# Two interleaved attention and MLP layers, forward and backward, on one core: the last dV products of the final stage two steps later, and all w2 and wo row blocks of the layer-0 backward products back on TensorE

## The chip, the core and the metric

The kernel runs on one core of one Trainium2 chip. The metric is the device time in microseconds of one execution. The core has TensorE (PE in the profile, with its weight loads listed apart as PEld), VectorE (DVE), ScalarE (ACT), GpSimd (POOL, which here issues the stores) and SyncE (SP, which issues the loads). Sixteen DMA engines move data between HBM and the on-chip memory; results of TensorE land in PSUM and have to be copied out ("evacuated") by VectorE or ScalarE.

## The reference

Two blocks, attention A and MLP B, are applied twice in turn (A, B, A, B) to one token for a batch of 2, with the same weights and the same key and value caches in both layers. The gradients for x, the caches and all weights and biases are asked for.

```python
def attn(x, K, V, wq, wo):            # x: (2, 1, 1024), 32 query heads, 4 kv heads, 16384 keys of 128
    q = (x @ wq) split into 32 heads
    p = softmax(q K^T / sqrt(128))
    return (p V, heads joined) @ wo

def mlp(x, w1, b1, w2, b2):           # 1024 -> 3584 -> 1024
    return gelu(layernorm(x) @ w1 + b1) @ w2 + b2

x = x + attn(layernorm(x), ...); x = x + mlp(layernorm(x), ...)     # layer 0
x = x + attn(layernorm(x), ...); x = x + mlp(layernorm(x), ...)     # layer 1
out_0 = x
out_1 .. out_9 = vjp(grad_out) for x, K, V, wq, wo, w1, b1, w2, b2
```

dK and dV have the size of the caches: 33.5 MB each, in bf16. They are the bulk of what is written.

## The kernel before

**Layout.** Vectors are kept as columns (128 partitions by number of 128-blocks by the batch of 2). Weights come in chunks of 1 MB (0.9 MB for w1), `LDW` = 4096 bf16 per partition, into a ring of 7 tiles (`NLD`); a tile is loaded again when all that read it are done. For one token a product is a matrix times two columns, so a weight block of 128x128 is the stationary operand and the moving operand is the two columns repeated to a width of 32 (`wide_in`). Where the product is with the transposed weight, the block is first transposed on TensorE (`PE.transpose`, eight blocks of 128x128 into one PSUM bank) and copied out by ScalarE or VectorE (`evac_bf16`). Who copies is decided when the program is built: `pick` compares two running sums of charged costs, `load["A"]` and `load["D"]`, and takes the engine with the smaller one; work that has a fixed engine is charged with `charge`.

**Stages.** The order of instructions on every engine is written out by hand (`manual_schedule`).

1. Layer 0 and layer 1 forward, up to about 460 us.
2. The layer-1 backward steps of w1 and wo, then `attn_bwd` (about 505 to 670 us). It runs in slots `s`; a slot handles a quarter of a chunk of 32x128 keys: transposes of V (`emit_T`), the products for dp (`score`), later the sums for dq. The last cache group is kept on chip, and its V tiles have to be turned in place before its own slots come (from the third group on). The deque `v_turns` holds these 16 turns (8 transposes and one evacuation each); before, one is taken in every third slot (`s % 3 == 2`).
3. The layer-0 backward products (about 670 to 755 us), run by the class `Ahead` for w2 (28 row blocks, `w2b`) and then for wo (32 row blocks, `wob`), with the w1 pass (`w_pass`) between them. `Ahead.row(j)` turns the row block, and for w2 first adds the forward products of layer 1 (L356); `Ahead.products(j)` makes the 8 products with the gradient columns (L372). In this kernel every fifth row block, j = 3, 8, 13, ... (`dotted`; 5 of w2 and 6 of wo), isn't turned. For these the gradient is spread first over all partitions (`Ahead.spread`, L328: 16 transposes of a broadcast column and two evacuations), and VectorE takes one row dot product for each of the two batch columns (`Dots.dot`, L332, with a charge of 1.15). The results go to `dp` and are put in afterwards: L805 in `mlp_hidden_bwd`, L831 in `do_delta`. TensorE's order around it: the sums of the layer norm's backward (`ln_bwd`, L178, with a few rows as a `hook` ahead of them), the spread, the remaining rows. Output 0 is transposed and stored in the midst of the w1 pass (`mid`, after the load of row block 4, L193 to L195).
4. `do_delta(0, ...)` gives the layer-0 gradient at the attention output. With it begins the last stage (about 755 us to the end): dK and dV for both layers, dq of layer 0, and all weight gradients. It runs in macro steps `m` of two slots. The 32 chunks stand in `chunks` (8 groups, four chunks each, `NCH` = 4, `NC` = 32). `k_at` and `v_at` give the macro step at which the dK and the dV product of a chunk begin; each has two halves (`kv_pair`, L1189: 8 matmuls into 4 PSUM banks and 4 evacuations of 128x512), one in that step and one in the next, and after the second half a store of 1 MB on GpSimd's queue. Before, chunk i has its dK begin at 2i - 4 (from i = 4 on) and its dV at 2i - 3, so both halves of both run in the same two steps, and `make_blks` turns the coefficients of both in one PSUM bank with one evacuation. The scores of the last chunk end at m = 56, the sums of its dq at m = 58, and its reduction runs at the end of m = 59; it calls `quarter`, which puts the last 16 weight-gradient units of wq (`dw_units`, L1048: one matmul of width 512 and one evacuation each, two stores) into `late` and the products with wq (L875) into `late_pe`. `step_fill` takes 5 such units per macro step.
5. `attn_in_bwd(0, ...)` and `col_to_row_f32` write output 1, a store of 4 KB, behind all of this.

Of the kernel before, what the change touches and what calls it, by code (L numbers as in the profile page):

```python
# [10 lines left out]
F32 = mybir.dt.float32  # L11
# [12 lines left out]
def kernel(  # L24
# [256 lines left out]
    def w_pass(W, n_in, n_out, name, xT_bf=None, gT_bf=None, mid=None):  # L281
# [10 lines left out]
        for j0, rb in w_chunks(n_in, n_out):  # L292
            wv = w_load(W, j0, rb, n_out)
            if mid is not None and j0 == 4:
                mid()
# [22 lines left out]
    class Dots:  # L318


        def __init__(self, name):
            self.rows = [ktp.tile([128, 2 * NB, 128], BF16, name=name, tag="blk", bufs=2) for _ in range(2)]
            self.junk = wrk.tile([128, D], BF16, name="junk", tag="rowout")

        def spread(self, b, col):
            tp = pt([128, 8, 128], BF16, "dotr")
            for o in range(8):
                PE.transpose(tp[:, o, :], col(o).to_broadcast([128, 128]), ident[:])  # L328
            evac_bf16(self.rows[b][:].rearrange("p a b -> p (a b)"), tp[:].rearrange("p a b -> p (a b)"), 1024)

        def dot(self, w, b, out):
            V.scalar_tensor_tensor(out=self.junk[:], in0=w, scalar=1.0, in1=self.rows[b][:].rearrange("p o d -> p (o d)"),  # L332
                                   op0=ALU.mult, op1=ALU.mult, accum_out=out)
            charge("D", 1.15)

    class Ahead:


        def __init__(self, W, n_in, name, xT_bf=None, fps=None):
            self.W, self.J, self.x, self.fps, self.name = W, n_in // 128, xT_bf, fps, name  # L340
            self.dotted = range(3, self.J, 5)
            self.dp = vec.tile([128, len(self.dotted), 2], F32, name=name + "_dp")
            self.chunks = list(w_chunks(n_in, D))
            self.rows = {}
# [7 lines left out]
        def row(self, j):  # L352
# [5 lines left out]
            if j not in self.dotted:  # L358
                turn(w, lambda: pt([128, 8, 128], BF16, "turn"))

        def spread(self, gT_bf):
            self.dd = Dots(self.name + "_g")
            for b in range(2):
                self.dd.spread(b, lambda o: gT_bf[:, o, b:b + 1])

        def products(self, j, out_ps, gT_bf):
            if j in self.dotted:
                for b in range(2):
                    self.dd.dot(self.rows[j], b, self.dp[:, self.dotted.index(j), b:b + 1])
                return  # L370
# [213 lines left out]
    def attn_bwd(l, do_bf, dqT, dn, groups, ahead):  # L584
# [13 lines left out]
        dd = Dots("dqb")  # L598
        dnp = vec.tile([128, HKV, DJ, 2], F32, name="dnp")

        def dot(kv, n, j, b):
            dd.dot(n[4][j - j % 4][:, j % 4, :], b, dnp[:, kv, j, b:b + 1])
            if b == 1:
                V.tensor_tensor(out=dn[:, j], in0=dn[:, j], in1=dnp[:, kv, j], op=ALU.add)

        def by_dots(kv):
# [4 lines left out]
            for b in range(2):  # L611
                wq_q.append(lambda b=b: dd.spread(b, lambda o: dq_all[:, kv * 8 + o, 2 * l + b:2 * l + b + 1]))
# [60 lines left out]
        while s < len(slots) + 2 or sch.busy():  # L673
            sch.s = s
            if s < len(slots):
# [3 lines left out]
                else:  # L679
# [3 lines left out]
                    if s % 3 == 2 and v_turns:  # L683
# [104 lines left out]
    def mlp_hidden_bwd(l, dhps, ahead=None):  # L788
# [15 lines left out]
        if ahead is not None:  # L804
            V.tensor_tensor(out=dh_all[:, 3:FJ:5, lsl(l)], in0=d1[:, 3:FJ:5], in1=ahead.dp[:], op=ALU.mult)  # L805
# [17 lines left out]
    def do_delta(l, dops, ahead=None):  # L823
        sv = saved[f"a{l}"]
        dof = wrk.tile([128, G, 8], F32, name="dof")
        for b in range(2):
            V.tensor_tensor(out=dof[:, b * HKV:(b + 1) * HKV, :].rearrange("p k r -> p (k r)"), in0=dops[:, :, b],
                            in1=sv["rbc"][:, b * HKV:(b + 1) * HKV, :].rearrange("p k r -> p (k r)"), op=ALU.mult)
            if ahead is not None:
                r_ = sv["rbc"][:, b * HKV:(b + 1) * HKV, :].rearrange("p k r -> p (k r)")  # L830
                V.tensor_tensor(out=dof[:, b * HKV:(b + 1) * HKV, :].rearrange("p k r -> p (k r)")[:, 3:HQ:5],  # L831
                                in0=ahead.dp[:, :, b], in1=r_[:, 3:HQ:5], op=ALU.mult)
# [97 lines left out]
    w2b.spread(gM_all[:, :, lsl(0)])  # L930
# [5 lines left out]
    mlp_hidden_bwd(0, pairs(dhps, FJ), w2b)  # L936
# [450 lines left out]
```

## Time and profile before

| what | value |
|---|---|
| time, median of 7 runs | 1173.96 us (1169.58 to 1176.09) |
| time of the profiled execution | 1174.01 us |
| span of the profiled execution | 1172.2 us, mean granted clock 0.825 |
| busy: PE / DVE / ACT | 961.4 us (82%) / 639.0 us (55%) / 562.6 us (48%) |
| moved by DMA | 449.30 MB, mean 383 GB/s |
| DMA share in the last stage, 830 to 1140 us | 1.00 or more in every 10 us |
| first instruction of `do_delta(0)` (L827) | 752.17 us |
| last dq ready (L1238) | 1147.39 us |
| store of output 1 issued (L195) | 1168.10 us |

The profiled execution took 0.05 us more than the median. Its span runs from the first to the last instruction, 1.8 us less than its time. A line of the timeline gives the start, the duration, the engine, the source line, what is written from what, the shapes, the number of instructions merged, and in brackets how long the engine had been idle and what released it.

### The profile page before, as it was taken

Reading aid. Unit: us, or ns where it says so; the run is one execution under the profiler, and the core shown is the slowest. Engines: PE = TensorE matmul, PEld = TensorE weight load, DVE = VectorE, ACT = ScalarE, POOL = GpSimd, SP = SyncE. Lnnn points to the kernel's source line nnn. Section 1 sums busy time; section 2 is a strip of 40 time slices with the busy share of each in tenths; the row PEclk is TensorE's granted clock in tenths of the full one; section 3 lists DMA queues with packets and bytes.
Section 4 is the critical chain, followed back from the end, with each engine's and each line's share of the span. In section 5 each row is a group of like instructions: output and inputs, shape, how many; then the busy total and the mean of one; then the engine's idle time right before and its main releaser. Section 6 shows DMA issues by size and latency. Waiting matters only on the chain. (4 is left out here: it accounts for less than half of the span.)

```text
span 1172.2 us, 39963 instructions
## 1 busy us (share of the span) xinstructions
PE 961.4 (82%) x17565; PEld 735.7 (63%) x17565; DVE 639.0 (55%) x1342; ACT 562.6 (48%) x1412; POOL 63.9 (5%) x113
## 2 busy tenths in 40 slices
PE   4888895488879876899986798688898988999786
PEld 3867673487767755887765697555555554555452
DVE  1535351133535423454844455758868867786774
ACT  0544351022535420344453454367767856686673
POOL 0000000000000000000000000001111111111111
PEclk9979795597989875999997889788859967796785
DMA  9999999998999989989899889668999999999995
GB/s 369 418 420 418 419 420 396 396 348 366 418 420 413 417 314 419 392 338 406 358 412 411 330 320 348 253 242 332 401 420 413 415 420 416 420 421 418 424 414 237
DMA packets 89130, 449.30 MB, mean 383 GB/s; under 512 B 7026, under 2 KB 7026, under 8 KB 49788
## 3 DMA queue, kind: packets, MB, share of 16 engines
q1 hardware_dynamic: 72204, 348.17, 74.3%
q0 software_dynamic: 16752, 98.59, 20.4%
q8 instruction: 137, 2.24, 0.8%
q14 instruction: 37, 0.30, 0.1%
HBM read 348.14 MB, written 98.58 MB: 381 GB/s over the span
## 5 line engine op out<-in xcount | busy, mean ns | idle before, releaser
L148 ACT COPY kT<-tp 128x512 int32<-128x512 int32 x206 | 121.0, 587 | 256.5 <-PE tp L411 242.2
L151 DVE COPY kT<-tp 128x1024 bf16<-128x1024 bf16 x162 | 110.8, 691 | 116.6 <-PE tp L411 105.0
L411 PE MATMUL tp<-ident,kv_K 128*128 128x128 bf16 x1728 | 145.7, 234 | 4.2 <-DMA kv_K<-in_A_k_cache_dram 4.0
L411 PEld LDWEIGHTS <-kv_K 128*128 128x128 bf16 x1728 | 110.6, 104 | 5.1 <-DMA kv_K<-in_A_k_cache_dram 4.5
L159 DVE CAST big<-xm 128x512 bf16<-128x512 f32 (+1 forms) x137 | 89.4, 686 | 26.1 <-PE xm L1189 11.3
L156 ACT CAST big<-xm 128x512 bf16<-128x512 f32 (+1 forms) x160 | 87.1, 593 | 24.8 <-PE xm L1048 13.5
L564 PEld LDWEIGHTS <-kT 128*128 128x128 bf16 x2048 | 76.6, 98 | 28.1 <-issue 22.4
L564 PE MATMUL sc<-qT_bf,kT 128*128 128x8 bf16 x2048 | 92.1, 171 | 0.4 <-issue 0.4
L411 PE MATMUL tp<-ident,kv_V 128*128 128x128 bf16 x864 | 71.1, 230 | 10.5 <-DMA kv_V<-in_A_v_cache_dram 8.8
L263 PE MATMUL wtp<-ident,wt 128*128 128x128 bf16 x928 | 76.5, 230 | 3.4 <-issue 2.1
L299 PEld LDWEIGHTS <-wt 128*128 128x128 bf16 x1696 | 49.0, 103 | 46.7 <-issue 15.0
L528 ACT ACTIVATE e_all<-sc,negm 128x64 bf16<-128x64 f32 x256 | 77.2, 345 | 1.1 <-DVE negm L523 1.0
L159 DVE CAST keepK<-xm 128x512 bf16<-128x512 f32 x94 | 61.1, 685 | 18.7 <-PE xm L1189 13.6
L443 PE MATMUL acc_all<-kv_V,e_all 128*16 128x256 bf16 x864 | 46.4, 295 | 28.7 <-DMA kv_V<-in_A_v_cache_dram 15.1
L148 ACT COPY wT<-wtp 128x512 int32<-128x512 int32 (+1 forms) x63 | 36.0, 576 | 67.8 <-PE wtp L263 59.3
L156 ACT CAST keepK<-xm 128x512 bf16<-128x512 f32 x103 | 55.6, 592 | 23.6 <-PE xm L1189 20.1
L151 DVE COPY wT<-wtp 128x1024 bf16<-128x1024 bf16 (+1 forms) x61 | 38.4, 634 | 50.3 <-PE wtp L263 46.0
L411 PEld LDWEIGHTS <-kv_V 128*128 128x128 bf16 x864 | 56.6, 103 | 11.6 <-DMA kv_V<-in_A_v_cache_dram 9.5
L156 ACT CAST keepV<-xm 128x512 bf16<-128x512 f32 (+1 forms) x98 | 52.9, 595 | 22.8 <-PE xm L1189 17.0
L263 PEld LDWEIGHTS <-wt 128*128 128x128 bf16 x928 | 58.3, 103 | 4.1 <-issue 2.7
L528 ACT ACTIVATION_READ_ACCUMULATOR e_all<-sc,negm 128x1 f32 x256 | 60.1, 235 | 0.0
L159 DVE CAST keepV<-xm 128x512 bf16<-128x512 f32 (+1 forms) x74 | 48.4, 685 | 17.4 <-PE xm L1189 14.4
(345 smaller groups left out, 1787.0 us busy)
## 6 DMA issues: line engine op xcount, KB each, us to landing
kv_K<-in_A_k_cache_dram SPq DMA_DIRECT2D x81, 1024.0 KB, 12.4
kv_V<-in_A_v_cache_dram SPq DMA_DIRECT2D x81, 1024.0 KB, 12.2
out_dram<-big POOLq DMA_DIRECT2D x36, 1024.0 KB, 18.4
wt<-in_A_wo_dram SPq DMA_DIRECT2D x32, 1024.0 KB, 10.7
wt<-in_B_w_dram SPq DMA_DIRECT2D x32, 896.0 KB, 14.3
out_dram<-keepK POOLq DMA_DIRECT2D x22, 1024.0 KB, 18.4
out_dram<-keepV POOLq DMA_DIRECT2D x18, 1024.0 KB, 18.2
wt<-in_A_wq_dram SPq DMA_DIRECT2D x16, 1024.0 KB, 9.2
```

Of the source, the lines that this page charges most:

```text
L148: S.copy(out=dst.bitcast(I32), in_=src.bitcast(I32))
L151: V.tensor_copy(out=dst, in_=src)
L156: S.copy(out=dst, in_=src)
L159: V.tensor_copy(out=dst, in_=src)
L263: PE.transpose(tp[:, o, :], wv[:, j, (o0 + o) * 128:(o0 + o + 1) * 128], ident[:])
L299: PE.matmul(fps[:, jo, :].rearrange("p (a b) -> p a b", b=2), lhsT=wv[:, j, jo * 128:(jo + 1) * 128], rhs=xT_bf[:, j0 + j, :].unsqueeze(1) ...
L411: PE.transpose(tp[:, j, :], cv[:, b * 8 + j, :], ident[:])
L443: PE.matmul(self.acc[cg:cg + 16, :], lhsT=coef(u), rhs=self.cv[:, t:t + 2, :].rearrange("p t d -> p (t d)"), start=False, stop=True, tile_ ...
L528: S.activation(out=e_all[:, g, f * half:(f + 1) * half, l, h, :], in_=sc[g][f][:, h, :].rearrange("p (a b) -> p a b", b=2), func=ACT.Exp, ...
L564: PE.matmul(sc[g][f][:, :, t % TH], lhsT=kT[:, j, :], rhs=q_bf[:, g, :], start=True, stop=True)
```

## The change

Five edits:

- `Ahead`: no row block is dotted. All 28 and 32 are turned and multiplied on TensorE; `spread`, the dots and the two places that put their results in (L805, L831) go.
- Output 0 is transposed and stored ahead of the w1 pass.
- `v_turns` takes a turn in every second slot.
- `v_at`: the dV products of chunks 28 to 31 begin two macro steps later, at 2i - 1. They then share `make_blks` with the dK of the next chunk; the dK of chunk 28 and the dV of chunk 31 have it for themselves, and the loop runs to m = 63 in place of 61.
- The helper class `Dots` goes; the dot products of `attn_bwd`, which stay, are written out there with the same instructions.

```diff
-    def w_pass(W, n_in, n_out, name, xT_bf=None, gT_bf=None, mid=None):
+    def w_pass(W, n_in, n_out, name, xT_bf=None, gT_bf=None):
...
-            if mid is not None and j0 == 4:
-                mid()
...
-            if j not in self.dotted:
-                turn(w, lambda: pt([128, 8, 128], BF16, "turn"))
-
-        def spread(self, gT_bf):
-            self.dd = Dots(self.name + "_g")
-            for b in range(2):
-                self.dd.spread(b, lambda o: gT_bf[:, o, b:b + 1])
+            turn(w, lambda: pt([128, 8, 128], BF16, "turn"))
 
         def products(self, j, out_ps, gT_bf):
-            if j in self.dotted:
-                for b in range(2):
-                    self.dd.dot(self.rows[j], b, self.dp[:, self.dotted.index(j), b:b + 1])
-                return
             for o in range(8):
...
-                    if s % 3 == 2 and v_turns:
+                    if s % 2 == 1 and v_turns:
                         v_turns.popleft()()
...
-        if ahead is not None:
-            V.tensor_tensor(out=dh_all[:, 3:FJ:5, lsl(l)], in0=d1[:, 3:FJ:5], in1=ahead.dp[:], op=ALU.mult)
...
-            if ahead is not None:
-                r_ = sv["rbc"][:, b * HKV:(b + 1) * HKV, :].rearrange("p k r -> p (k r)")
-                V.tensor_tensor(out=dof[:, b * HKV:(b + 1) * HKV, :].rearrange("p k r -> p (k r)")[:, 3:HQ:5],
-                                in0=ahead.dp[:, :, b], in1=r_[:, 3:HQ:5], op=ALU.mult)
...
-    w2b.spread(gM_all[:, :, lsl(0)])
     some(rest, 6)
...
-    mlp_hidden_bwd(0, pairs(dhps, FJ), w2b)
+    mlp_hidden_bwd(0, pairs(dhps, FJ))
     x4 = mlp_out(1, fps[:, 0:DJ * WIDE].rearrange("p (j b) -> p j b", b=WIDE)[:, :, 0:2])
+    col_to_row_f32(x4, DJ, out_0.rearrange("b s d -> (b s) d"), "o0")
     sv = saved["m0"]
-    _, dmps = w_pass(B_w1, D, F, "dm_ps", gT_bf=dh_all[:, :, lsl(0)],
-                     mid=lambda: col_to_row_f32(x4, DJ, out_0.rearrange("b s d -> (b s) d"), "o0"))
+    _, dmps = w_pass(B_w1, D, F, "dm_ps", gT_bf=dh_all[:, :, lsl(0)])
...
-    wob.spread(gA_all[:, :, lsl(0)])
...
-    do_delta(0, pairs(dops, HQ), wob)
+    do_delta(0, pairs(dops, HQ))
...
-    v_at = {2 * i - 3: i for i in range(2, NC)}
+    v_at = {2 * i - 3 + (2 if i >= NC - NCH else 0): i for i in range(2, NC)}
```

## The prediction

> **What bounds the kernel now.** I began with the page's 40 slices and then cut the span into windows of 10 us. From 830 to 1140 us the DMA share is 1.00 or more: nothing inside that stretch pays, but all of it waits for what comes before. The share sags from 660 to 820 us and after 1140 us, and the change touches both places. In the windows below (length, busy time of PE, PEld, DVE, ACT, POOL, granted clock, DMA share, GB/s) the reader is to see VectorE full in the second one, where TensorE is not.
>
> ```profile
> 730.00:740.00 10.00, 9.50 (x175) 9.05 (x173) 6.62 (x11) 5.24 (x9) 0.00 (x0) 0.83 0.13 20
> 740.00:750.00 10.00, 7.30 (x202) 6.87 (x198) 9.72 (x17) 4.72 (x9) 0.00 (x0) 1.00 0.99 376
> ```
>
> The timeline of that stage says what ends last: TensorE's last products end at 748.49 us, VectorE's last dot at 751.1 us, and the first step of `do_delta` comes at 752.17 us. TensorE waits 4.78 us. It also stands still for 1.5 us ahead of each spread.
>
> ```profile
> 677.60 1.89 PE L328 MATMUL dotr<-ident,gM_all 128*128 128x128 bf16 x16 [1.51 <-DVE gM_all L929]
> ...
> 729.51 1.07 PE L328 MATMUL dotr<-ident,gA_all 128*128 128x128 bf16 x16 [1.51 <-DVE gA_all L951]
> ...
> 730.92 3.46 PE L315 MATMUL turn<-ident,wt 128*128 128x128 bf16 x32 [0.34 <-DVE wob_g L151]
> ...
> 747.28 1.21 PE L372 MATMUL wob_b<-gA_all,wt 128*128 128x32 bf16 x32
> ...
> 749.89 1.22 DVE L332 SCALAR_TENSOR_TENSOR junk<-wt,wob_g 128x1024 bf16<-128x1024 bf16 x1
> ...
> 752.17 0.17 DVE L827 TENSOR_TENSOR dof<-wob_b,rbc 128x32 f32<-128x32 f32 x1
> ...
> 753.27 0.69 PE L178 MATMUL dl_ps<-dprod,onesf 128*128 128x64 f32 x2 [4.78 <-DVE dprod L836]
> ```
>
> The clock matters here. Windows of 1 us show it fall or rise at 673.1, 683.4, 731.2 and 734.6 us, all multiples of 3.41 us apart; so I read activity in windows of that length. The second one here, with 28% of spread and a few transposes, is followed by half clock; the first, with 40 transposes and 4 small matmuls, by full.
>
> ```profile
> 724.33:727.75 3.42, 2.91 (x44) 2.62 (x43) 2.55 (x11) 1.61 (x3) 0.00 (x0) 1.00 1.05 386
> 727.75:731.16 3.41, 1.56 (x25) 1.36 (x24) 1.99 (x9) 1.13 (x2) 0.00 (x0) 1.00 0.68 252
> 731.16:734.57 3.41, 3.41 (x45) 3.32 (x43) 1.38 (x2) 0.79 (x3) 0.00 (x0) 0.50 0.00 1
> ```
>
> Last, GpSimd's queue in the tail. The reader is to see 12 us without a store, around the last dq (1147.39 us), and the last four 1 MB stores behind it.
>
> ```profile
> 1143.30 0.53 POOL L1012 DMA_DIRECT2D out_dram<-keepK  x1 [1.35 <-ACT blk L148]
> 1155.85 0.53 POOL L1012 DMA_DIRECT2D out_dram<-keepV  x1 [12.02 <-DVE keepV L159]
> 1157.73 0.53 POOL L1012 DMA_DIRECT2D out_dram<-keepK  x1 [1.35 <-ACT big L156]
> 1159.58 0.77 POOL L1012 DMA_DIRECT2D out_dram<-big  x1 [1.31 <-ACT big L156]
> 1162.62 0.77 POOL L1012 DMA_DIRECT2D out_dram<-big  x1 [2.27 <-ACT big L156]
> ```
>
> **Prices.** From the starts between 684.64 and 685.49 us, at full clock: a turn 0.44 us of TensorE, 8 products 0.21, a w2 row's forward matmuls 0.20. At half clock a turn with forward matmuls takes 1.07 (681.63 to 682.70) and a turn alone 0.87 (3.46/4). An evacuation is 0.59 on ScalarE or 0.69 on VectorE; a turned row every 0.85 us leaves these two room. A dot is 1.27 us of VectorE with its read-out.
>
> **w2, 5 rows back.** TensorE ends the layer norm's sum at 676.1 us, then waits and spreads until 679.2. After the change the rows 2 to 7 follow at once, as they need no gradient. Before, they take until 684.44. After, six turned rows at 1.07 take until 682.5 if the clock rises at 683.4 as it did; if the now busy window from 676.55 brings it up at 679.97, they take until 681.5. Gain 1.9 to 2.9. The loop then gets four more turns (8, 13, 18, 23: 1.76) and five more products (1.05), and 0.5 more if the clock is late: loss 2.8 to 3.3. Sum -0.1 to +1.4. I take 0.1, because a busy window was followed by full clock each time above. The w2 chunks do not bind: five have landed a median 5.6 us after their issue near 665 us. Row 3 now frees its tile by a product instead of a dot, so w1's first load (690.56 us) goes out earlier.
>
> **Output 0.** Before, 8 transposes and two casts hold TensorE from 711.09 to 712.90 (1.81), and it waits 0.49 for `dh_all` at 702.47. After, w1's transposes wait behind the output's, and these behind three small VectorE steps (0.75 after the last product): 0.75 + 1.81 against 2.30, +0.3. The derivative's steps (700.46 to 702.2, 1.75) no longer stand behind dots; their cover is the last 1.7 us of products, without which this costs up to +1.7. The low end is -0.2. The 4 KB store has GpSimd's queue for itself.
>
> **wo, 6 rows back.** Row 3's turn delays the first sum by 0.4. Rows 8 to 11 then start at 728.4 instead of 730.92, without a spread to wait for. Their evacuations on VectorE wait for the layer norm's end (729.45), so I let row 12 end at 731.4 at full clock, or at 732.8 at 0.87 each, against 734.4: -3.0 to -1.5. Behind it four more turns (1.76) and six more products (1.26): +3.0. TensorE ends at 748.5 to 750.0. I take 748.6. The eighth wo chunk waits for the tile of rows 0 to 3, today for a dot (issue at 738.52, first used 744.29); now for a product at about 734, so it does not bind. Then VectorE: the dots are gone, and the two 0.5 us clears of PSUM fall ahead of the last products. `do_delta` starts at 748.7 instead of 752.17, -3.5, and saves 0.3 for the two L831 steps. Sum of this stage -3.8, ends -3.9 and -2.4.
>
> The Trainium skill, "TensorE: Matmul & The Clock Gate", section "Part 4: PE-mode transpose", speaks against all this: it says that transposes don't count as busy for the clock. If so, the 11 turns would be paid at half clock, 0.43 us more each, and the sum would be 4.7 us higher. The row of 724.33, where 44 instructions of which 40 are transposes are followed by full clock, says otherwise, and I go by the row.
>
> **Shares of the copies.** The dots' charges make the builder give every evacuation between 758 and 771 us to ScalarE: four casts in a row take 2.05, where split ones take 1.29 (771.37). Without them three half-pairs each shrink by 0.8. TensorE shows only 0.5 us of wait for these, so -0.5; ends 0 and -2.4.
>
> **Turns of V.** The same 16 turns; five move ahead of slot 32. Their cover: the DMA share is 0.99 to 1.03 from 520 to 560 us and TensorE later waits 9.2 us for V between 600 and 655, which swallows a small delay. I take 0. Without cover 5 x 0.44 = +2.2; if they relieve the sag at 560 to 570 (share 0.69), -2.
>
> **The last dV products.** Steps m = 53 and 54 (1119.76 to 1127.33) lose one half-pair each: 0.6 us of TensorE each (1122.03 to 1122.63, 1125.85 to 1126.46), or, as the copying engines are full there, up to 1.2 (four casts on two engines). I take 0.8 each: -1.6, by which the last dq comes earlier. Behind dq two half-pairs more: K and V at 1153.19 take 3.24 until the next unit, so +3.2, less 0.4 because units of 0.44 overlap casts: +2.8. Chunk 31's own transposes (0.4) and evacuation (0.4) hide beside units: 0, else +0.8. Its store goes in ahead of the last wq store, five instead of four MB behind 1155.85. Four drained until 1168, at 2.9 per MB; the extra one begins while units still run, and output 1's store ends last as today. Behind the half-pairs wait only the last units and the layer norm of output 1. Sum +1.2, ends -1.2 and +2.8.
>
> **Sum.** 0.1 + 0.3 - 3.8 - 0.5 + 0 + 1.2 = -2.7. The profiled execution took 1174.01, 0.05 above the median: 1171.3.
>
> **Rivals.**
> 1. TensorE becomes the bound at half clock. If the window with rows 8 to 12 and one more in each of w2 and wo stay at half clock (each 3.41 us, 1.7 lost), w2 costs 1.4 + 1.7, output 0 0.3, and TensorE ends the wo rows at 750.0 + 1.7, so `do_delta` gains 0.7 at most: +2.7 before the copies' -0.5 and the tail's +1.2, 1177.4. For it: half clock from 673.1 to 683.4 with TensorE busy most of the time. Against: the windows above. It decides from `do_delta` starting later than some 750.5, which leaves no gain over the tail.
> 2. The early gain is swallowed: the long stretch at full DMA share has its bytes, and an earlier start only lengthens the wait for stores; only the tail shows, 1175.2. For: share 1.00 for 310 us. Against: the first store comes at 767 us, and 770 to 820 has shares of 0.64 to 0.96, so the bytes start earlier too.
> 3. The dq does not come earlier, so that the change doesn't do what it says: if steps 53 and 54 are held by transposes and scores, only the +2.8 is left: 1174.01 - 3.9 + 2.8 = 1172.9. For: TensorE is near full at 1120 to 1130.
>
> **Chances.** Less than 0.2% (2.35 us) can't be told from no change, so faster means below 1171.6. Forecast 0.46; rival 1 0.28; rivals 2 and 3 together 0.26. Faster 0.46, same 0.26, slower 0.28. The likeliest case's own range is 1168 to 1173.5; with rivals 1 and 2, 1167 to 1177.5.
>
> **What would show it.** Right: no L328 for gM_all and gA_all and no wait before it; L827 near 749; casts on both engines from 758; DMA share unchanged in mid-stage; last dq (L1238) 5 us earlier than 1147.39 and the time from there to the end 2.8 longer. Wrong: half clock through rows 8 to 20 of wo; waits of TensorE for V before 600 us; L827 later than 751; a tail more than 4 us longer.

## The result, and the profile after

The changed kernel takes 1180.0 us (median of 31 runs, 1174.3 to 1185.6) against 1173.5 us for the kernel before on the same chip (73 runs). The ratio is 1.0049, 95% interval 1.0038 to 1.0060: slower by 5.8 us (4.5 to 7.0). The prediction was 1171.3 us.

The profiled execution took 1180.26 us, with a span of 1178.4 us against 1172.2. I cut both spans at the same events (layer 0's dO is the start of L834 before and L806 after, the "first dq" the first of this stage):

| stretch | before | after | difference |
|---|---|---|---|
| start to layer 1's dO (no instruction of it changed) | 508.6 | 511.4 | +2.8 |
| to the last dn of layer 1 | 165.0 | 164.8 | -0.2 |
| to layer 0's dO (w2, output 0, w1, layer norm, wo) | 79.2 | 78.0 | -1.2 |
| to the first dq | 22.2 | 21.7 | -0.5 |
| to the second dq | 67.7 | 71.3 | +3.6 |
| to the seventh dq | 270.1 | 269.3 | -0.8 |
| to the last dq | 34.5 | 32.3 | -2.2 |
| to the end of the span | 24.8 | 29.5 | +4.7 |

Not every row of this is the change. The first one lies ahead of every edit and took between 508.0 and 512.1 us in the profiles of all 20 kernels. The fifth was between 69.7 and 72.8 us in the 19 other profiles, so the 67.7 before was low by itself. What can be put down to the change is in three rows: the layer stage, which gained 1.2 us instead of 3.4, and the two around the last dq.

The windows over the layer stage of the changed kernel, to be read beside those of 730 to 750 us before (columns: length, busy time of PE, PEld, DVE, ACT and POOL, granted clock, DMA share, GB/s):

```profile
724.00:734.00 10.00, 8.57 (x166) 7.89 (x164) 5.96 (x20) 4.10 (x7) 0.00 (x0) 1.00 1.04 387
734.00:744.00 10.00, 9.04 (x194) 8.59 (x191) 5.62 (x14) 4.32 (x8) 0.00 (x0) 1.00 0.42 126
744.00:754.00 10.00, 9.42 (x256) 9.13 (x254) 4.30 (x7) 3.30 (x6) 0.00 (x0) 1.00 1.03 399
```

VectorE is no longer the full engine, TensorE is, and the clock is 1.00 throughout. The spreads (L328) of both gradients are gone, with their two waits of 1.51 us. The end of that stage, in the timeline of the changed kernel:

```profile
750.91 0.69 DVE L151 COPY wt<-turn 128x1024 bf16<-128x1024 bf16 x1 [2.92 <-ACT wt L148]
...
752.10 1.32 PE L340 MATMUL wob_b<-gA_all,wt 128*128 128x32 bf16 x40
...
752.30 0.69 DVE L151 COPY wt<-turn 128x1024 bf16<-128x1024 bf16 x1 [0.70 <-PE turn L313]
...
753.10 1.03 DVE L932 MEMSET tpm<- 128x512 f32 x2
754.03 0.22 DVE L803 TENSOR_TENSOR dof<-wob_b,rbc 128x32 f32<-128x32 f32 x2
...
754.67 0.43 PE L178 MATMUL dl_ps<-dprod,onesf 128*128 128x64 f32 x2 [1.25 <-DVE dprod L808]
```

TensorE's last products end at 753.42 us. `do_delta` (now L803) starts 0.6 us later, because the two clears of PSUM stand in front of it on VectorE, and these start only when VectorE has done the last row's evacuation (752.30). TensorE's wait is 1.25 us where it was 4.78.

The stage lost more ahead of it. The layer norm between w1 and wo, from `dm_sb` (L917) to `gA_all` (L922), took 7.7 us against 6.0. In the timeline:

```profile
727.72 1.05 PE L313 MATMUL turn<-ident,wt 128*128 128x128 bf16 x16
...
728.33 0.17 DVE L223 TENSOR_REDUCE lb_s<-lb_t 128x2 f32<-128x16 f32 x1
728.50 0.69 DVE L151 COPY wt<-turn 128x1024 bf16<-128x1024 bf16 x1
...
729.25 1.05 PE L313 MATMUL turn<-ident,wt 128*128 128x128 bf16 x16 [0.47 <-DVE wt L151]
...
730.14 0.34 PE L178 MATMUL lb_ps<-lb_s,onesf 128*128 128x4 f32 x2
```

The sums are ready at 728.50 us, but the matmul that adds them over the partitions starts at 730.14, behind four turns. The third turn waits for the PSUM tile of the first, whose evacuation on VectorE stands behind the sums. Before, row 3 was a dot and needed no turn.

GpSimd's queue at the tail, to be read beside the five stores shown before:

```profile
1144.62 0.53 POOL L982 DMA_DIRECT2D out_dram<-keepxK  x1 [1.56 <-DVE keepxK L159]
1157.38 0.53 POOL L982 DMA_DIRECT2D out_dram<-keepV  x1 [12.23 <-DVE keepV L159]
1159.16 0.53 POOL L982 DMA_DIRECT2D out_dram<-keepK  x1 [1.25 <-ACT blkv L148]
1160.84 0.77 POOL L982 DMA_DIRECT2D out_dram<-keepK  x1 [1.15 <-ACT keepK L156]
1167.69 0.53 POOL L982 DMA_DIRECT2D out_dram<-keepxV  x1 [6.08 <-DVE keepxV L159]
1168.80 0.77 POOL L982 DMA_DIRECT2D out_dram<-big  x1 [0.58 <-issue]
1174.34 0.53 POOL L195 DMA_DIRECT2D out_dram<-o_row  x1 [4.77 <-DVE o_row L194]
```

The last dq is ready at 1148.92 us, 1.5 later than before, where 5 earlier was predicted. The last wq store goes out at 1168.80 against 1162.62, output 1 at 1174.34 against 1168.10.

### The profile page after: what moved, and what is told of

Read it like the earlier page. It is cut to its first block, busy times and chain, and to the rows that moved or that the text cites. A ratio compares the mean times of both kernels' runs of the same rounds, so it can differ in the third digit from the quotient of the medians.

```text
span 1178.4 us, 40223 instructions
## 1 busy us (share of the span) xinstructions
PE 974.3 (83%) x17709; PEld 745.2 (63%) x17709; DVE 628.2 (53%) x1320; ACT 554.0 (47%) x1395; POOL 63.9 (5%) x113
## 5 line engine op out<-in xcount | busy, mean ns | idle before, releaser
L159 DVE CAST big<-xm 128x512 bf16<-128x512 f32 x137 | 89.3, 685 | 27.4 <-PE xm L1159 13.4
L532 PEld LDWEIGHTS <-kT 128*128 128x128 bf16 x2048 | 76.6, 98 | 28.9 <-issue 23.2
L156 ACT CAST big<-xm 128x512 bf16<-128x512 f32 x152 | 82.4, 595 | 22.3 <-PE xm L1159 10.9
L263 PE MATMUL wtp<-ident,wt 128*128 128x128 bf16 x928 | 79.1, 235 | 4.7 <-issue 3.5
L148 ACT COPY wT<-wtp 128x512 int32<-128x512 int32 (+1 forms) x60 | 34.5, 576 | 72.8 <-PE wtp L263 63.5
```

The lines of the kernel that those rows point to most:

```text
L148: S.copy(out=dst.bitcast(I32), in_=src.bitcast(I32))
L156: S.copy(out=dst, in_=src)
L159: V.tensor_copy(out=dst, in_=src)
L263: PE.transpose(tp[:, o, :], wv[:, j, (o0 + o) * 128:(o0 + o + 1) * 128], ident[:])
L532: PE.matmul(sc[g][f][:, :, t % TH], lhsT=kT[:, j, :], rhs=q_bf[:, g, :], start=True, stop=True)
```

## The experiments

They stand in the order in which they were run, most with 12 executions beside the kernel before on the same chip (5 to 7 for the four named e11 to e14 below); ratios are to that kernel. Differences between two of them carry an interval made of both (the root of the sum of the squared half widths). The runs are called e1 to e18 in this order. The letters of the theories are those of the expectations: A, the tail pays; B, TensorE's rows pay; C, no single part; later D to U.

**The parts alone.** First, the last four dV chunks two steps later, in the kernel before:

```diff
-    v_at = {2 * i - 3: i for i in range(2, NC)}
+    v_at = {2 * i - 3 + (2 if i >= NC - NCH else 0): i for i in range(2, NC)}
```

> The kernel before with the dV products of the last group two macro steps later, nothing else. Theory A (the tail pays): in the trace of the changed kernel the time from the last dq to the end grew from 24.8 to 29.5 us, and the last dq came some 0.6 us earlier counted from the step that prepares chunk 28; so +3 to +4.5 us, and the same two extra half-pairs of about 1.9 us each between the last weight-gradient units. Theory B (the tail pays little, as predicted, and the TensorE rows cost the rest): at most +1.5 us. Theory C (most of the loss belongs to no single part): +1 to +2 here, and no single part reaches +3.

1176.2 us, 1.0014 [0.9995, 1.0034]. From the last dq to the end 28.6 us (24.8 before), and from the seventh dq to the last 32.0. In eleven profiles with dV at its old steps the latter took 33.0 to 34.9 us (mean 34.0), in five with it two steps later 32.0 to 32.3. So 4.5 us of tail (28.6 to 29.5, mean 29.3) stand against 1.7 us of gain in front (a mean of 32.2 against 34.0): about +2.8 by the traces.

The turns of V, every second slot instead of every third:

```diff
-                    if s % 3 == 2 and v_turns:
+                    if s % 2 == 1 and v_turns:
```

> The kernel before with one turn of V in every second slot instead of every third, nothing else. Theory A: 0 +- 1 us; the dq of the first groups may come 1 to 4 us later, as in the changed kernel (542.4 against 538.2 us for the first), and the last dq of layer 1 not later than the start of the stage is. Theory C: +1 to +3, because the load queue loses time at 520 to 530 us (share 0.85 in the changed kernel, 1.00 before) that the stage never gets back.

1174.2 us, 1.0006 [0.9990, 1.0022]: nothing that can be told from zero.

All eleven row blocks of w2 and wo on TensorE, output 0 still inside the w1 pass:

```diff
-            if j not in self.dotted:
-                turn(w, lambda: pt([128, 8, 128], BF16, "turn"))
+            turn(w, lambda: pt([128, 8, 128], BF16, "turn"))
...
-            if j in self.dotted:
-                for b in range(2):
-                    self.dd.dot(self.rows[j], b, self.dp[:, self.dotted.index(j), b:b + 1])
-                return
...
-    w2b.spread(gM_all[:, :, lsl(0)])
...
-    wob.spread(gA_all[:, :, lsl(0)])
...
```

> The kernel before with all row blocks of w2 and wo turned and multiplied on TensorE and no dots there; output 0 stays in the midst of the w1 pass. Theory A: -3 to -1 us, with the start of do_delta 2 to 4 us earlier counted from the end of the layer-1 attention. Theory B: +2 to +4 us, with TensorE as the bound of both stages. Theory C: +1 to +2.

1173.3 us, 1.0003 [0.9980, 1.0026]. The stretch from the last dn to layer 0's dO took 75.5 us in the profile, 3.7 less than before, and the time did not show it.

Output 0 ahead of the w1 pass, with the dots kept:

```diff
-    _, dmps = w_pass(B_w1, D, F, "dm_ps", gT_bf=dh_all[:, :, lsl(0)],
-                     mid=lambda: col_to_row_f32(x4, DJ, out_0.rearrange("b s d -> (b s) d"), "o0"))
+    col_to_row_f32(x4, DJ, out_0.rearrange("b s d -> (b s) d"), "o0")
+    _, dmps = w_pass(B_w1, D, F, "dm_ps", gT_bf=dh_all[:, :, lsl(0)])
```

> The kernel before with output 0 transposed and stored ahead of the w1 pass, nothing else. The dots stay, so the derivative's small VectorE steps stand behind them as before. Theory A: +0.5 to +2.5 us, as TensorE stands still for these steps (5.0 us from the last w2 products to the first w1 transposes were seen for the changed kernel, where one counts the output's own 1.8). The prediction's own term: +0.3. Theory C: +1 to +2.

1175.1 us, 1.0018 [1.0004, 1.0033]. The four parts add up to 0.41% (0.04 to 0.78), where the whole change costs 0.49%. No part alone carries it.

**The change with one part taken back, and dV moved by other distances.** The changed kernel with dV on its old steps:

```diff
-    v_at = {2 * i - 3 + (2 if i >= NC - NCH else 0): i for i in range(2, NC)}
+    v_at = {2 * i - 3: i for i in range(2, NC)}
```

> The changed kernel with the last four dV chunks back on their old steps (turns of V, output 0 first and all rows on TensorE kept). The profile of the dV edit alone showed 28.6 us from the last dq to the end against 24.8 us before, and some 1 to 2 us less in front of it. Theory A (the tail costs about 2 us net and sits on top of the rest): about 2 us under the changed kernel's 1180.0, so 1177 to 1178, ratio to the kernel before 1.002 to 1.004; the time from the last dq to the end is back at 24.8 us. Theory D (two of the edits only hurt together: TensorE has no cover left when output 0 stands between the products and the pass of w1): the tail makes little of it, the ratio stays at 1.003 to 1.005.

1176.3 us, 1.0020 [1.0005, 1.0035]; 0.29% (0.10 to 0.48) under the changed kernel. The tail is back at 24.8 us. Theory A holds for dV, and what is left, +2.3 us, belongs to the rest. What the tail pays for is seen in the timelines of TensorE, this run's first, the changed kernel's second:

```profile
1156.15 1.18 PE L1159 MATMUL xm<-QmV,blk 32*128 32x256 bf16 x8 [0.67 <-DVE keepV L159]
1157.81 5.28 PE L1018 MATMUL xm<-rowsA,rowsB 4*128 4x512 bf16 x12 [0.49 <-ACT keepK L156]
1163.82 0.56 PE L178 MATMUL lb_ps<-lb_s,onesf 128*128 128x4 f32 x2 [0.73 <-DVE lb_s L223]
```

```profile
1158.07 2.29 PE L1018 MATMUL xm<-rowsA,rowsB 4*128 4x512 bf16 x5
1159.75 1.22 PE L1159 MATMUL xm<-QmV,blkv 32*128 32x256 bf16 x3
1161.13 0.58 PE L1159 MATMUL xm<-QmV,blkv 32*128 32x256 bf16 x5 [0.17 <-DVE big L159]
1162.26 2.35 PE L1018 MATMUL xm<-rowsA,rowsB 4*128 4x512 bf16 x5 [0.54 <-ACT keepxV L156]
1164.00 1.22 PE L1159 MATMUL xm<-QmV,blkv 32*128 32x256 bf16 x3
1165.39 0.58 PE L1159 MATMUL xm<-QmV,blkv 32*128 32x256 bf16 x5 [0.17 <-DVE big L159]
1166.51 1.00 PE L1018 MATMUL xm<-rowsA,rowsB 4*128 4x512 bf16 x2 [0.54 <-ACT keepxV L156]
1168.67 0.56 PE L178 MATMUL lb_ps<-lb_s,onesf 128*128 128x4 f32 x2 [1.16 <-DVE lb_s L223]
```

Twelve units of the weight gradients run in 5.28 us there. Here two half pairs stand among them and the same units take 9.44 us (1158.07 to 1167.51): 2.08 for a half pair, whose 8 matmuls stop 0.17 us for a free PSUM tile and whose successor waits 0.54 us for the copies. The granted clock is 0.50 in every 1 us window from 1147 us to the end in both runs, so the clock is not the difference. The last layer norm then waits 0.43 us longer. The two and these 0.43 make 4.59 of the 4.7 us.

The changed kernel with output 0 back behind the first four row blocks of the w1 pass:

```diff
-    col_to_row_f32(x4, DJ, out_0.rearrange("b s d -> (b s) d"), "o0")
-    _, dmps = w_pass(B_w1, D, F, "dm_ps", gT_bf=dh_all[:, :, lsl(0)])
+    _, dmps = w_pass(B_w1, D, F, "dm_ps", gT_bf=dh_all[:, :, lsl(0)],
+                     mid=lambda: col_to_row_f32(x4, DJ, out_0.rearrange("b s d -> (b s) d"), "o0"))
...
```

> The changed kernel with output 0 back inside the pass of w1 (behind its first four row blocks). In the profiles the stretch from the last dn of layer 1 to layer 0's dO took 79.2 us before, 75.5 us with all rows on TensorE alone, 79.6 us with output 0 first alone and 78.0 us with both. Theory D (output 0 first costs about 2.5 us when the rows are on TensorE, where it cost 0.4 us beside the dot products): that stretch is back at 75 to 76 us and the time is 2 to 3 us under the changed kernel's 1180.0, ratio to before 1.002 to 1.003. Theory A alone: stretch at 78, ratio 1.005 as in the changed kernel.

1178.4 us, 1.0038 [1.0020, 1.0057]: 0.11% (-0.11 to 0.33) under the changed kernel. The stretch was 77.3 us, not 75 to 76, so theory D is not borne out. By the times output 0 costs 1.3 us here (-1.3 to +3.9) and 2.1 us with the dots (0.5 to 3.9, e4).

dV of the last group one step earlier, in the kernel before:

```diff
-    v_at = {2 * i - 3: i for i in range(2, NC)}
+    v_at = {2 * i - 3 - (1 if i >= NC - NCH else 0): i for i in range(2, NC)}
```

> The kernel before with the dV products of the last group one macro step earlier instead of two later (steps 52, 54, 56, 58). Theory A (products behind the last dq are paid in full at half clock, 1.87 us for a half pair, those in front of it in part): from the last dq to the end about 1.9 us less than 24.8 us, some 0.5 to 1 us given back in front; 0.5 to 1.5 us faster, ratio 0.999. Theory C (what stands in front of the last dq is as full as what stands behind it): no change, ratio 1.000, the time only moved from behind the last dq to in front of it.

1172.8 us, 0.9999 [0.9980, 1.0018]. The tail was 23.0 us (1.8 less) and the stretch in front of it 35.2 (1.2 over the mean of 34.0). By the traces a gain of 0.6 us, which the times neither show nor exclude.

dV of the last group four steps later (the same line with `+ (4 if ...)`):

> The kernel before with the dV products of the last group four macro steps later (57, 59, 61, 63) instead of two: twice the moved distance. Theory A (each half pair behind the last dq costs 1.87 us): from the last dq to the end about 32.3 us, 7.5 us over the kernel before, with 2 to 3 us less in front of it; ratio 1.003 to 1.005. Theory C: the time in front shrinks by as much as the tail grows, or the pairs fill idle time of the tail; ratio under 1.002.

1177.7 us, 1.0040 [1.0028, 1.0051]. Tail 32.9 us, 8.1 over before; in front 30.1, 3.9 less than the mean. Net +4.2 by the trace, +4.7 by the times. Each half pair put behind the last dq costs about 2 us there and returns about 1 in front.

**What wo and w2 do, and whether an earlier start counts.** Only wo's six row blocks on TensorE, in the kernel before:

```diff
-            self.dotted = range(3, self.J, 5)
+            self.dotted = range(3, self.J, 5) if name != "wob" else range(0)
...
-    wob.spread(gA_all[:, :, lsl(0)])
...
-    do_delta(0, pairs(dops, HQ), wob)
+    do_delta(0, pairs(dops, HQ))
```

> The kernel before with the six row blocks of wo alone back on TensorE (their spread and dots gone; w2 keeps its dots, output 0 and dV stay). So far the stretch from gA_all to layer 0's dO took 18.7 us in every kernel with wo's rows on TensorE and 22.6 to 23.6 us with the dots, and the two layer-norm steps ahead of it 7.7 us against 6.0. Theory P (what the layer gains reaches the end): about 4.3 - 1.7 = 2.6 us faster, ratio 0.9978. Theory R (rival 2 of the prediction: the last stage is held by its DMA, so an earlier start is lost there): that local gain in the profile, and a ratio of 0.9995 to 1.0010.

1172.2 us, 0.9994 [0.9981, 1.0006]. In the profile the stretch from `gA_all` to dO was 18.7 us and the layer norm 7.1, together 3.4 us less than in the profiles with all dots (18.7 against a mean of 23.2, 7.1 against 6.0); in the time 0.7 us (-0.7 to 2.2).

Only w2's five (the same edit for w2, with its spread and its results taken out):

> The kernel before with the five row blocks of w2 alone back on TensorE. The stretch from gM_all to dh_all took 22.7 to 26.3 us (mean 24.7) with all rows on TensorE and 22.7 to 24.8 (mean 23.8) with the dots. Theory P: about 0.9 us slower, ratio 1.0008. Theory R: a loss reaches the end too where it delays the loads of the last stage; 1.000 to 1.001. If it is over 1.002, the w2 rows and not output 0 or dV are what the change loses by.

1174.4 us, 1.0006 [0.9989, 1.0022]. From the last dn to the first writing of `dh_all` the kernels with w2's rows on TensorE took 26.4 to 29.0 us (mean 27.7), those with dots 26.4 to 28.5 (27.1): about +0.6.

The dots of wo left out. This kernel leaves six of the 32 row blocks out of layer 0's dO, with zeros in their place, and drops the dots' charges with them:

```diff
+            V.memset(self.dp[:], 0.0)
...
             if j in self.dotted:
-                for b in range(2):
+                for b in range(2 if self.name != "wob" else 0):
```

> The kernel before with the twelve dots of wo left out (their place in layer 0's dO is filled with zeros; spread, turns and products of the other rows stay): a pure gain ahead of do_delta, with nothing put on TensorE. By the profile before, TensorE ends about 748.6 us and the dots' tail on VectorE holds do_delta to 752.2, so do_delta starts about 3.5 us earlier. Theory P: 3.5 us faster, ratio 0.997. Theory R: 0.999 to 1.000 although do_delta starts 3.5 us earlier.

1167.4 us, 0.9957 [0.9944, 0.9970]: 5.0 us faster, with dO about 4 us earlier.

The two dots of row block 28 done three times (which adds four charges too):

```diff
+    for _ in range(2):
+        wob.products(28, dops, gA_all[:, :, lsl(0)])
     do_delta(0, pairs(dops, HQ), wob)
```

> The kernel before with the two dots of row block 28 of wo done three times instead of once, ahead of do_delta (4 more dots of 1.15 us on VectorE): do_delta starts 4.6 us later and nothing else is added. Theory P: 4.6 us slower, ratio 1.0039. Theory R, if the last stage is full of DMA from its start: a part of the delay is caught up, ratio 1.000 to 1.002. A full loss here with no gain in the run without dots would mean that the stage takes a later start in full but cannot use an earlier one.

1179.2 us, 1.0058 [1.0039, 1.0077]: 6.8 us slower. Its timeline shows the added dots and nothing else in front of `do_delta`:

```profile
750.84 1.02 DVE L962 MEMSET tpm<- 128x512 f32 x2
751.77 1.20 DVE L332 SCALAR_TENSOR_TENSOR junk<-wt,wob_g 128x1024 bf16<-128x1024 bf16 x1
...
755.55 1.22 DVE L332 SCALAR_TENSOR_TENSOR junk<-wt,wob_g 128x1024 bf16<-128x1024 bf16 x1
...
756.70 0.18 DVE L827 TENSOR_TENSOR dof<-wob_b,rbc 128x32 f32<-128x32 f32 x1
```

In both directions the shift passes to the end in full, within the intervals (3.5 to 6.6 us for about 4 earlier, 4.6 to 9.1 for about 5 later). Theory R, the prediction's rival 2, falls: the last stage is full of DMA from 830 us on, and an earlier or a later start of `do_delta` reaches its end all the same. So wo's rows had to show their gain, unless they lose something elsewhere.

**What wo's rows lose, and what output 0 loses.** The run of wo alone, with the planner's charges of the dots kept though no dot is there. A charge moves no work by itself; it makes the builder give the next copies to the other engine.

```diff
+            if self.name == "wob" and j in range(3, self.J, 5):
+                charge("D", 2 * 1.15)
             for o in range(8):
                 PE.matmul(wide_out(out_ps, 2 * j), lhsT=self.rows[j][:, o * 128:(o + 1) * 128],
```

> The six rows of wo on TensorE as in the run of wo alone (ratio 0.9994), but the planner's twelve charges of 1.15 us to VectorE kept, so that the copies after the stage are shared as before. Theory S (the rows gain 2.6 us and the loss sits in the shares of the copies): 0.9975 to 0.9985. Theory T (the loss is TensorE's work itself): 0.9990 to 1.0000, as without the charges.

1168.5 us, 0.9965 [0.9952, 0.9978]: faster than the kernel before, and 0.29% (0.11 to 0.47) under wo's rows without the charges, though on another chip (e18 below repeats the pair on one chip). The windows of the 12 us ahead of dO, without the charges first, with them second:

```profile
737.33:749.33 12.00, 11.13 (x298) 10.76 (x294) 5.40 (x11) 4.10 (x7) 0.00 (x0) 1.00 1.03 394
```

```profile
734.91:746.91 12.00, 11.59 (x319) 11.46 (x316) 1.79 (x5) 7.98 (x14) 0.00 (x0) 1.00 1.01 382
```

VectorE's share (third) falls from 5.40 to 1.79 us, ScalarE takes it, and the stretch from `gA_all` to dO takes 17.7 us instead of 18.7.

The run of wo alone with the turns and products of the six row blocks left out as well (their part of dO is zero, one clear of the PSUM bank is added, and no charge is kept):

```diff
-            if j not in self.dotted:
+            if j not in self.dotted and not (self.name == "wob" and j in range(3, self.J, 5)):
                 turn(w, lambda: pt([128, 8, 128], BF16, "turn"))
...
+            if self.name == "wob" and j in range(3, self.J, 5):
+                return
```

> The run of wo alone with the turns and products of the six rows left out as well (no dots and no TensorE work for them; their place in layer 0's dO is zero). By the profile six rows on TensorE cost 6 x 0.65 = 3.9 us. Theory T: about 4 to 5 us faster than wo's rows on TensorE, ratio 0.995 to 0.996, and no better than leaving out the dots alone (0.9957), since VectorE's and TensorE's ends then lie together. Theory S: no more than 3.9 us under 0.9994, ratio 0.9965.

1166.6 us, 0.9946 [0.9924, 0.9968], 15.6 us from `gA_all` to dO. That is 0.48% (0.23 to 0.73), or 5.6 us, under the same kernel with the rows (3.1 us plus a layer norm back at 6.0 in the profiles). It fits theory T in size; but the charged run has all of TensorE's work too and keeps 4.1 us, so T alone doesn't explain e9. On the same chip it is 0.19% (-0.07 to 0.45), 2.2 us, under the charged run.

wo's rows on TensorE with dV one step earlier (the edits of e9 and e7 together):

> wo's rows on TensorE and the last group's dV products one macro step earlier: the two edits that did not lose alone (0.9994 and 0.9999). If they add: 0.9990 to 0.9995, at best 1 us faster than the kernel before. A clear gain (under 0.998) would mean that an end of the last stage that comes earlier helps the one through the other.

1168.7 us, 0.9975 [0.9955, 0.9995], more than the two alone add up to, within their intervals. So e9's 0.9994 was probably at the unlucky end of its own.

The changed kernel with the derivative's independent steps split off into `mlp_hidden_d1` and put ahead of w2's products:

```diff
...
+    d1 = mlp_hidden_d1(0)
     dhps = px([128, 512], F32, "w2b_b")
...
-    mlp_hidden_bwd(0, pairs(dhps, FJ))
+    mlp_hidden_bwd(0, pairs(dhps, FJ), d1)
```

> The changed kernel with the steps of the activation's derivative that need no product issued on VectorE ahead of w2's products, instead of behind them. Theory U (output 0 first loses because nothing covers the derivative: TensorE's gap of 1.14 us ahead of output 0's transposes and the later start of w1's turns): the stretch from gM_all to dh_all 1.2 to 1.7 us shorter, and the time 1 to 2 us under the changed kernel's 1180.0, ratio to before 1.0035 to 1.004. Rival: w1's turns stand behind output 0 and are the bound, so the derivative is hidden all the same: ratio 1.005.

1176.4 us, 1.0034 [1.0011, 1.0057]; 0.15% (-0.10 to 0.40) under the changed kernel. TensorE's idle time ahead of output 0's transposes is 0.60 us instead of 1.14, so only 0.5 us was uncovered. But the w1 transposes behind output 0 took 1.50 us where they took 2.72 in the changed kernel. That is the clock, and not this edit: the run without the dV edit has the same instructions here as the changed kernel and differs in the same way. In each of the two profiles all rises and falls near here lie whole multiples of 3.41 us apart, so I cut the stretch there. First the run without the dV edit, then the changed kernel:

```profile
699.32:702.73 3.41, 2.61 (x94) 2.51 (x90) 2.29 (x11) 0.58 (x1) 0.00 (x0) 1.00 0.81 272
702.73:706.14 3.41, 2.30 (x31) 1.87 (x32) 1.78 (x5) 0.58 (x1) 0.08 (x1) 1.00 0.99 410
706.14:709.55 3.41, 3.41 (x88) 3.33 (x86) 1.99 (x4) 1.76 (x3) 0.63 (x1) 1.00 1.04 408
```

```profile
704.26:707.67 3.41, 1.49 (x26) 0.96 (x23) 1.95 (x9) 0.00 (x0) 0.00 (x0) 1.00 0.83 341
707.67:711.08 3.41, 3.41 (x47) 3.41 (x45) 1.43 (x3) 1.17 (x2) 0.70 (x1) 0.50 1.02 423
```

The same stretch with little work on TensorE is cut in two by the first profile's grid (2.61 and 2.30 us busy, full clock after both) and falls into one window in the second (1.49 us busy, half clock for the next 3.41 us). Of five profiles with output 0 first, three show the half clock (24 transposes in 2.72, 2.53 and 2.77 us), two do not (1.50). The other two with the half clock, e4 and e17, have 1.84 and 1.49 us busy in the window ahead of it; e16, without, is cut in two as e5 is (2.88 and 2.58). Of the 15 profiles with output 0 inside the w1 pass three have 0.9 to 2.4 us of half clock at the start of the pass.

**The charges in the changed kernel, and the two gains together.** First the changed kernel with the charges of e13:

> The changed kernel with the planner's charges of the wo dots kept (2.3 us to VectorE at each sixth of a row block; no instruction is added). Theory S (with the charges gone, copies of the wo stage stand on VectorE ahead of do_delta and the last stage begins later): the stretch from gA_all to layer 0's dO 17.7 us instead of 18.7, VectorE's busy time in its second half near 1.8 us instead of 5.4, and 1 to 3.4 us under the changed kernel, ratio to before 1.002 to 1.004. Rival (the difference between 0.9994 and 0.9965 was one of chips): ratio 1.004 to 1.005 although the stretch is shorter.

1177.8 us, 1.0024 [0.9999, 1.0049]: 0.25% (-0.02 to 0.52) under the changed kernel. The stretch from `gA_all` to dO is 17.7 us. The clears still wait for the last evacuations, but these are ScalarE's now: the first clear runs ahead of the last one, and `do_delta` starts 0.14 us after TensorE's last product (751.48) instead of 0.6:

```profile
750.59 0.48 DVE L934 MEMSET tpm<- 128x512 f32 x1 [8.94 <-ACT wt L148]
751.23 0.48 DVE L934 MEMSET tpm<- 128x512 f32 x1 [0.16 <-ACT wt L148]
751.62 0.22 DVE L805 TENSOR_TENSOR dof<-wob_b,rbc 128x32 f32<-128x32 f32 x2
```

Then the kernel before with wo's rows on TensorE, the charges, and dV one step earlier:

> The kernel before with wo's rows on TensorE, the charges kept, and the last group's dV products one macro step earlier. If the gains add (0.9965 with the charges; 0.9999 for dV earlier): 0.9955 to 0.997, 3.5 to 5 us faster. If the gain of the charged run was one of its chip: 0.998 to 0.9995.

1169.1 us, 0.9952 [0.9933, 0.9971]: 5.6 us faster than the kernel before, the best kernel of this study that computes everything. Its tail is 23.4 us, `gA_all` to dO 17.8. Beside e15, run on the same chip, it differs by the charges alone: 0.23% (-0.05 to 0.51), 2.7 us. With e17 against the changed kernel that is 0.24% (0.05 to 0.43), 2.8 us (0.6 to 5.1): so the charges are worth something without e13 and e9, which stood on two chips.

## Why the prediction was wrong

The forecast was 2.7 us faster; the change is 5.8 us slower. Three terms of its sum failed. The price of the last dV products was too small: the tail grew by 4.7 us where +2.8 was put. The term for the shares of the copies had the wrong sign: dropping the dots' charges costs 1.0 us ahead of `do_delta` in the traces, where 0.5 behind it was to be gained. And wo's rows gained 2.8 us instead of 3.8 (that 1.0 is in it), as the layer norm ahead of them became 1.7 us longer.

**The last dV products: mis-sized, and the largest miss that the traces show.** The mechanism was right, and so was the gain in front (1.6 predicted, 1.7 found). The tail was put at "+2.8" and is +4.7 in the profile after, +4.5 on the mean. The step that failed took the price of two half pairs from "K and V at 1153.19", 3.24 us, and subtracted 0.4 for overlap. There a half pair of V follows one of K at once, and with their waits they take 1.57 and 1.67 us. Alone between units a half pair takes 2.08 us, 0.9 more for the two, the 0.4 for overlap is not found, and the final layer norm waits 0.43 us longer: together the missing 1.8 us. That the neighbour covers a part of the copies is the likely reason for the lower price, and no run tried it. Net about +2.8 instead of +1.2; by the times +1.6 (e1) and +3.4 (changed kernel against e5). The text named "a tail more than 4 us longer" as a sign of being wrong, and it was that.

**wo: -3.8 predicted, -2.8 found in the traces** (-4.5 from `gA_all` to dO, +1.7 in the layer norm). Two steps failed. "Row 3's turn delays the first sum by 0.4": the turns stood ahead of both layer norms' sums, held by evacuations that VectorE did behind its own reductions, +1.7. And "the two clears fall ahead of the last products": they waited on VectorE behind the last evacuation. Keeping the charges took 1.0 us off the stretch. That TensorE does the rows at full clock, and that the 4.78 us of waiting vanishes, was right; the wait became 1.25.

**Shares of the copies: -0.5 predicted, the sign was wrong.** I looked at the casts behind `do_delta` only, where the stretch to the first dq shows no more than 0.5 us of gain. But the same charges steered the evacuations in front of `do_delta`. Without them VectorE gets half of these, the engine that has `do_delta` to do: 1.0 us in the traces (18.7 us from `gA_all` to dO in seven profiles without the charges, 17.7 or 17.8 in three with them), and 2.7 to 3.4 us in the times of three pairs (e13 against e9, on two chips; e17 against the changed kernel and e18 against e15, each with zero just inside its interval). Where more than the 1.0 us would come from I have not found. Against more than 1.0 us stand e11 and e14, which drop the charges too and pass on what they gain ahead of dO in full, within their intervals.

**Output 0: +0.3 predicted, +1.3 (e6, with zero inside its interval) and +2.1 (e4) by the times.** The cover was in part missing: the derivative's steps stand behind the last evacuation on VectorE, which costs 0.4 to 0.5 us. Another part I had not thought of: in three of five profiles the clock is halved behind this idle stretch, some +1.2 each time. That was the rule of rival 1 at a place where I had not applied it.

**w2 and the turns of V:** +0.1 predicted and about +0.6 found; 0 predicted and +0.7 us (-1.2 to +2.6) measured. Within their ranges.

**The rivals.** Rival 1 (half clock through wo's rows) did not happen: every window there is at 1.00. Rival 2 (the gain is swallowed) is refuted by e11 and e12. Rival 3 (the dq doesn't come earlier) neither: the stretch in front of it shrank by 1.7 us. `do_delta` did start at 754.03 us. The last dn of layer 1 came 2.6 us later than before, ahead of all this; without that it would be 751.4, still behind the 750.5 of rival 1 and the 751 that the prediction named as a sign of being wrong, but at full clock. The Trainium skill ("TensorE: Matmul & The Clock Gate", "Part 4: PE-mode transpose") says that a transpose doesn't count as busy for the clock the way a matmul does. This has no support here: the layer norm's turns and wo's rows in the changed kernel run at 1.00 from 724 to 754 us. The prediction's row for that was read rightly in its first line; the "28%" of its second isn't the row's, which has TensorE busy for 1.56 of 3.41 us, 46%.

**The sum.** With the sizes found, w2 +0.6, output 0 +0.4 to 1.6, wo -2.8, copies behind `do_delta` -0.2, dV +2.8, turns 0 to +0.5: between +0.8 and +2.5 us by stretches, where the times say +5.8 (4.5 to 7.0). Some 3 to 5 us are thus not placed. The parts' own times add to 0.41% or 4.8 us, so no interplay of parts is needed. Taken back from the changed kernel one by one, the dV edit (3.4 us, e5) and the lost charges (2.9 us, e17) are about the whole loss by the times, with wide intervals; no run took back both. If the charges cost that much, some 2 of the unplaced 3 to 5 us are theirs. Another 1.3 us may lie in the first row of the table: it took 510.4 to 511.4 us (mean 510.8) in the changed kernel and the four runs made from it, against a mean of 509.5 in the 15 others (508.0 to 512.1), and no run tells whether the change does that. The stretches of a single profile scatter by 1 to 2 us, and what lies below that in the 270 us of full DMA can't be seen in one. That stays open.

## What to carry to other kernels

A dummy charge in a load balancer is a scheduling decision: when the work that it stands for goes away, look at which engine the copies next to the critical step now land on, and try keeping the bias if that engine has the critical step. Price work that is moved into a tail by a lone instance of it with its waits, not by one that stands beside its like. And test the passing-on of a gain before reasoning about it: one run with a dummy delay and one with the work left out told in two runs what shares of busy time could not.

## What the runs showed of the hardware that was not expected

The clock behind one and the same stretch of low TensorE activity was 1.00 in one execution and 0.50 for 3.41 us in another, with the same instructions there (e5 and the changed kernel). So its fall is not a function of the instructions alone, but also of where they lie in time: near here all rises and falls of a profile lie on one grid of 3.41 us. In the five profiles with output 0 first the half clock came where one window of the grid took nearly the whole stretch (1.49 to 1.84 us busy), and not where the grid cut it in two (2.30 to 2.88 us busy). A sharp border doesn't follow: in the changed kernel the window from 697.43 to 700.84 us had 1.86 us busy, and full clock came after it. Some 1.2 us at such a place is chance in any single profile.

TensorE also stops one to three times in w2's products with nothing to wait for that the profile shows ("issue"): 0.7 to 2.1 us each, 26 stops over 0.6 us in 17 of the 20 profiles, with the dots (0.74 to 2.13) as without (0.79 to 1.71). Each of them ends 2.2 to 2.6 us (one 3.3) after the start of the last packet ahead of it on the DMA queue that the profile's page calls "instruction" (q8), and so do, at 2.1 to 2.7 us, all but one of the 158 such stops from 20 us on in the 20 profiles. So TensorE most likely waits for its own instructions there; no run varied this. In w2's products the stops add up to 3.8 us in the profile after, 0.3 before and 0 to 2.9 in the others, so a single pair of profiles can differ by this much.
